# Moving the fallback path ahead of the main path, and queries and V per group, in a grouped-query attention kernel

## Chip, cores, metric

One core of one Trainium2 chip. The metric is device microseconds of one execution, median over several; faster or slower needs 2%. Engines: PE does matmuls, ACT the exps, DVE evicts results, POOL copies V, SP issues the DMAs. The "issue" of a DMA is the time that its record on SP lasts; it has "landed" when its data are there.

## The reference

```python
B, Hq, Hkv, Sq, Sk, D = 16, 32, 8, 288, 512, 128          # bf16
k = jnp.repeat(k, 4, axis=1); v = jnp.repeat(v, 4, axis=1)
scores = jnp.einsum("bhqd,bhkd->bhqk", q, k) * D ** -0.5
p = softmax(scores)
return jnp.einsum("bhqk,bhkd->bhqd", p, v)
```

There are 128 groups (16 x 8): each has 1152 query rows (9 tiles of 128), 512 keys, and takes three steps.

## The kernel before

The main path takes exp without subtracting the maximum. It gathers the range of the row sums, and at the end a flag says whether they are in bounds. If not, all engines run a general path (the fallback; 11,150 PE instructions in the built program) that subtracts it. Here the flag is 0.

```python
def op_load(u, part=None):                # u: unit of UG = 4 groups, 3 slots
    ...                                   # wait until the slot's scores are done
    eng.dma_start_transpose(kt_sb[...], k_v[(gg + g0) * P:(gg + g1) * P])
    eng.dma_start_transpose(qt_sb[...], q_v[(gg + g0) * P:(gg + g1) * P])
    if part != 0:
        ...
        eng.dma_start(vd_sb[:, sl], v_v[:, gg:gg + UG])

def op_s(n):    # a step of PE: 4 matmuls, 1536 columns of scores, 2 buffers in PSUM
    ...
def op_exp(n):  # ACT: exp of 128x1536
    ...
def op_pv(r):   # PE, NC + 1 = 4 steps later: 12 matmuls 128x129 (V and a ones column)
    ...
def op_vc(u):   # POOL: spreads a unit's V (128x2048) beside the ones column
    ...
sp.append((-10.0, lambda: op_load(0, 0)))          # group 0
sp.append((-9.0, lambda: op_load(0, 1)))           # groups 1 to 3
for u in range(1, NU):
    sp.append((-8.0 if u < NSLOT else NC * UG * (u - NSLOT + 1) + LAG, lambda u=u: op_load(u)))
for g in range(NG):
    sp.append((NC * (g + 1) + LAG + 1.5, lambda g=g: op_store(g)))
sp.sort(key=lambda x: x[0])                        # the order of SP's queue
...
def guarded(key, first=None):                      # after the main path, on each engine
    def body(eng):
        eng.wait_ge(sem["s_flag"], 1)
        reg = eng.alloc_register("bad_" + key)
        eng.load(reg, flag_i[:])
        with eng.If_ne(reg, 0):                    # taken jump over the general path
            ...
            fns[key](eng)
```

All DMAs are issued by SP in one queue.

## Time and profile before

| what | value |
|---|---|
| time, median of the first 3 runs | 545.61 us (544.48 to 546.3) |
| profiled span | 542.7 us |
| PE, ACT busy | 524.6 us (97%), 522.0 us (96%) |
| start of the first exp / of the last | 7.37 / 531.40 us |
| from the end of the flag's CAST to the end | 4.9 us |

Two engines at 96% and 97% leave a few microseconds at each end. So one reads when the exp stream starts, whether it is broken, and what follows the flag; the prediction shows those lines. In a windows row the DMA share can pass 1 (1.09 from 20 to 40 us): it is the sum of packet times over 16 engines.

### The profile page before, as it was taken

The page shows a single profiled execution, that of the slowest core. Times are in us where ns is not written, and L with a number is a line of the kernel's source. Part 1 is how long each engine was busy: PE and PEld are TensorE (multiplying, and loading weights), DVE is VectorE, ACT ScalarE, POOL GpSimd, SP SyncE. Part 2 cuts the span into 40 slices and gives each one's busy share as a digit, 9 for nine tenths or more (in the row PEclk, how much of TensorE's full clock was granted, in tenths as well). Part 3 has the DMA queues.
Part 4 walks back from the last instruction along what each step waited for, and adds up shares of the span by engine and source line. Part 5 has one row for each costly group of instructions (what it writes and reads, how often), then busy time and mean ns, then how long its engine had stood idle before and what let it go on. Part 6 is the DMA issues. An engine that isn't in the chain of part 4 may idle for free.

```text
span 542.7 us, 14127 instructions
## 1 busy us (share of the span) xinstructions
PE 524.6 (97%) x6146; PEld 411.1 (76%) x6146; DVE 288.2 (53%) x807; ACT 522.0 (96%) x386; POOL 61.3 (11%) x37
## 2 busy tenths in 40 slices
PE   4799999999999999999999999999999999999994
PEld 1677777777777777777777777777777777777773
DVE  0355555555555555555555555555555555555554
ACT  4799999999999999999999999999999999999992
POOL 0211111011111011111011111001111011111000
PEclk9899999999999999999999999999999999999998
DMA  8999899988879989789998979988888998888211
GB/s 169 214 255 263 212 210 229 206 205 182 236 213 223 213 182 230 205 215 221 192 223 190 229 213 220 246 161 234 183 226 217 198 220 196 223 209 222 88 67 72
DMA packets 250501, 110.05 MB, mean 203 GB/s; under 512 B 217664, under 2 KB 234048, under 8 KB 250432
## 3 DMA queue, kind: packets, MB, share of 16 engines
q1 hardware_dynamic: 250432, 109.07, 84.4%
q8 instruction: 50, 0.82, 0.7%
q14 instruction: 19, 0.16, 0.1%
HBM read 16.78 MB, written 37.75 MB: 100 GB/s over the span
## 4 chain that ended last, share of the span: by engine, by line
PE 95%; SPq 2%; DMA 1%; DVE 1%; POOL 0%; issue 0%
PE ps_o L449 50%; PE ps_s L431 46%; SPq L393 1%; DMA vd_sb<-in_v_dram 1%; SPq L390 1%; POOL v_sb L473 0%; DVE o_sb L493 0%; DVE rl_sb L481 0%; PE ps_s L534 0%; DVE ck_sb L560 0%; DVE ck_sb L566 0%; DVE ck_sb L563 0%; DVE st_sb L505 0%; DVE flag_i L569 0%; DVE st_sb L503 0%
## 5 line engine op out<-in xcount | busy, mean ns | idle before, releaser
L462 ACT ACTIVATE pt_sb<-ps_s 128x1536 bf16<-128x1536 f32 x384 | 520.5, 1451 | 10.1 <-PE ps_s L431 10.0
L449 PEld LDWEIGHTS ps_o<-v_sb,pt_sb 128*128 128x128 bf16 x4608 | 301.0, 98 | 58.7 <-POOL v_sb L473 3.3
L449 PE MATMUL ps_o<-v_sb,pt_sb 128*128 128x129 bf16 x4608 | 333.8, 221 | 3.3 <-POOL v_sb L473 2.9
L431 PE MATMUL ps_s<-qt_sb,kt_sb 128*128 128x512 bf16 (+3 forms) x1536 | 314.1, 327 | 7.9 <-DMA qt_sb<-in_q_dram 7.6
L493 DVE TENSOR_TENSOR o_sb<-ps_o,rl_sb 128x384 bf16<-128x384 f32 x384 | 213.9, 557 | 13.5 <-DVE rl_sb L481 0.3
L481 DVE RECIPROCAL rl_sb<-ps_o 128x3 f32<-128x3 f32 x384 | 69.3, 181 | 234.7 <-PE ps_o L449 234.7
L431 PEld LDWEIGHTS ps_s<-qt_sb,kt_sb 128*128 128x128 bf16 x1536 | 130.0, 98 | 65.7 <-DMA qt_sb<-in_q_dram 5.9
L473 POOL COPY v_sb<-vd_sb 128x2048 bf16<-128x2048 bf16 x32 | 60.7, 1898 | 439.7 <-DMA vd_sb<-in_v_dram 285.7
L505 DVE TENSOR_REDUCE st_sb<-rl_sb 128x1 f32<-128x72 f32 x16 | 3.5, 218 | 0.0
L503 DVE TENSOR_REDUCE st_sb<-rl_sb 128x1 f32<-128x72 f32 x16 | 3.5, 217 | 0.0
L540 ACT ACT_TABLE_LOAD x1 | 1.3, 1283 | 0.8 <-PEq L608 0.8
L534 PE MATMUL ps_s<-ck_sb,one_f 128*1 128x1 f32 x2 | 0.2, 164 | 1.8 <-DVE ck_sb L566 1.8
L534 PEld LDWEIGHTS ps_s<-ck_sb,one_f 128*1 128x1 f32 x2 | 0.1, 82 | 2.0 <-DVE ck_sb L566 2.0
L552 DVE MEMSET dum<- 128x2 f32 x1 | 0.1, 60 | 0.9 <-PEq L608 0.9
L546 POOL MEMSET v_sb<- 128x48 bf16 x1 | 0.3, 312 | 0.3 <-POOLq L608 0.3
L569 DVE CAST flag_i<-ps_s 1x1 int32<-1x1 f32 x1 | 0.1, 145 | 0.3 <-PE ps_s L534 0.3
L540 ACT ACTIVATE dum<-dum 128x1 f32<-128x1 f32 x1 | 0.2, 203 | 0.0
L560 DVE TENSOR_REDUCE ck_sb<-st_sb 128x1 f32<-128x16 f32 x1 | 0.2, 170 | 0.0
L566 DVE SCALAR_TENSOR_TENSOR ck_sb<-ck_sb 128x1 f32<-128x1 f32 x1 | 0.2, 158 | 0.0
L563 DVE TENSOR_SCALAR ck_sb<-ck_sb 128x1 f32<-128x1 f32 x1 | 0.2, 153 | 0.0
L562 DVE TENSOR_REDUCE ck_sb<-st_sb 128x1 f32<-128x16 f32 x1 | 0.2, 159 | 0.0
L608 POOL MEMSET const-float32-0.0<- 128x1 f32 x1 | 0.1, 100 | 0.3 <-issue 0.3
(4 smaller groups left out, 0.4 us busy)
## 6 DMA issues: line engine op xcount, KB each, us to landing
out_dram<-o_sb SPq DMA_DIRECT2D x128, 288.0 KB, 4.9
vd_sb<-in_v_dram SPq DMA_DIRECT2D x32, 512.0 KB, 4.8
kt_sb<-in_k_dram SPq DMA_TRANSPOSE x33, 5.1
qt_sb<-in_q_dram SPq DMA_TRANSPOSE x33, 8.4
```

The costliest lines, as they stand in the source:

```text
L390: eng.dma_start_transpose(kt_sb[:, sl, :, g0:g1].rearrange("d j g p -> d j (g p)"), k_v[(gg + g0) * P:(gg + g1) * P]).then_inc(sk, 16)
L393: eng.dma_start_transpose(qt_sb[:, sl, :, g0:g1].rearrange("d t g p -> d t (g p)"), q_v[(gg + g0) * P:(gg + g1) * P]).then_inc(sq, 16)
L431: ins = emit(eng, waits if x == 0 else [], lambda: eng.matmul(ps_s[:, n % 2, a - i * CH:b - i * CH], kt_sb[:, sl, j, gi, :], qt_sb[:, sl, ...
L449: ins = emit(eng, waits if a == 0 and j == 0 else [], lambda: eng.matmul(ps_o[:, r % 2, a * DV:(a + 1) * DV], w, v_sb[:, sl, gi * NJ + j, ...
L462: emit(eng, waits, lambda: eng.activation(pt_sb[:, g % NPT, i * CH:(i + 1) * CH], ps_s[:, n % 2], ACTF.Exp, scale=scale)).then_inc(sem["s_ ...
L473: emit(eng, waits, lambda: eng.tensor_copy(v_sb[:, sl, :, 0:D], vd_sb[:, sl].rearrange("p g (j d) -> p (g j) d", d=D))).then_inc(sem["s_vc ...
L481: emit(eng, [("s_pv", r + 1)], lambda: eng.reciprocal(rl_sb[:, 3 * r:3 * r + 3], src.rearrange("p a e -> p (a e)"))).then_inc(sem["s_rc"], 1)
L493: emit(eng, waits, lambda: eng.tensor_tensor(out=o_sb[:, g % NO, t0:t0 + 3, :], in0=src, in1=rl_sb[:, 3 * r:3 * r + 3].unsqueeze(2).broadc ...
L503: emit(eng, [("s_rc", (b + 1) * w // 3)], lambda: eng.tensor_reduce(st_sb[:, 0, b:b + 1], rl_sb[:, b * w:(b + 1) * w], AX.X, ALU.max))
L505: eng.tensor_reduce(st_sb[:, 1, b:b + 1], rl_sb[:, b * w:(b + 1) * w], AX.X, ALU.min).then_inc(sem["s_stat"], 1)
L534: emit(eng, [("s_bad", 1)], lambda: eng.matmul(ps_s[0:1, 0, 0:1], one_f[:], ck_sb[:, 3:4], start=True, stop=True)).then_inc(sem["s_bad"], 1)
L540: emit(eng, [("s_one", 1)], lambda: eng.activation(dum[:, 1:2], dum[:, 0:1], ACTF.Exp))
```

## The change

The intent: (1) put the general path ahead of the main path in each engine's stream, so that the engines jump at the start, while they wait for data anyway, and run straight to the end after the flag; (2) transpose queries per group (12 slots) and spread V per group, so that work starts with less loaded; (3) let SP read the flag before it waits for the last stores.

```diff
+        def behind_general(key, first=None):
+            def body(eng):
+                home[key] = nc.cur_bb
+                eng.br("main_" + key)
+                with nc.body("general_" + key):
+                    ...
+                    fns[key](eng)
+                    eng.br("done_" + key)
+                nc.switch_bb("main_" + key)
+        def end(eng, key):
+            eng.wait_ge(sem["s_flag"], 1)
+            eng.load(reg, flag_i[:])
+            if key == "sp":
+                ...                        # the waits for the last stores
+            eng.br_ne(reg, 0, "general_" + key, "done_" + key)
-        qt_sb = ... [P, NSLOT, NT, UG, P]
+        qt_sb = ... [P, NQ, NT, P]          # NQ = 12
-        def op_load(u, part=None):          # K, queries and V of a unit
+        def op_kv(u, part=None):            # K and V of a unit
+        def op_q(g):                        # queries of one group
+            if g >= NQ: ...                 # wait for the scores of group g - 12
+            eng.dma_start_transpose(qt_sb[:, g % NQ], q_v[g * P:(g + 1) * P])
+            sp.append((NC * UG * (u - 1) - 1.0 if u < NSLOT else ..., lambda u=u: op_kv(u)))
+            sp.append((-9.5 if g == 0 else -8.5 + 0.1 * g if g < UG else NC * (g - NQ + 1) + 1.2, lambda g=g: op_q(g)))
-            for u in range(NU): op_vc(u)
+            for g in range(NG): op_vc(g)
```

More of the change, by code (lines that the diff above doesn't have):

```diff
@@ L314, in bass_standalone__gqa_softmax__near_ridge_kernel @@
     NSLOT = 3
+    NQ = 12
     NPT = 3
@@ L333, in bass_standalone__gqa_softmax__near_ridge_kernel @@
         block = es.enter_context(nc.Block())
+        S("s_go")
+        gen = ExitStack()
+        fns = general_path(nc, gen, q, k, v, out, sem["s_go"])
+        gen.close()
+        home = {}
+        def behind_general(key, first=None):
+            def body(eng):
+                if first:
+                    first(eng)
+                home[key] = nc.cur_bb
+                eng.br("main_" + key)
+                with nc.body("general_" + key):
+                    if key == "sp":
+                        eng.sem_inc(sem["s_go"], 1)
+                    fns[key](eng)
+                    eng.br("done_" + key)
+                nc.switch_bb("main_" + key)
+            return body
+        def end(eng, key):
+            eng.wait_ge(sem["s_flag"], 1)
+            reg = eng.alloc_register("bad_" + key)
+            eng.load(reg, flag_i[:])
+            if key == "sp":
+                for g in range(NG - NO, NG):
+                    for (s, n) in need(eng, [("s_o%d" % (g % NO), 16 * (g // NO + 1))]):
+                        eng.wait_ge(s, n)
+            eng.br_ne(reg, 0, "general_" + key, "done_" + key)
+            nc.switch_bb("done_" + key, parent=home[key])
         main = ExitStack()
@@ L336, in bass_standalone__gqa_softmax__near_ridge_kernel @@
         v_sb = main.enter_context(nc.sbuf_tensor("v_sb", [P, NSLOT, UG * NJ, VP], BF16))
-        qt_sb = main.enter_context(nc.sbuf_tensor("qt_sb", [P, NSLOT, NT, UG, P], BF16))
+        qt_sb = main.enter_context(nc.sbuf_tensor("qt_sb", [P, NQ, NT, P], BF16))
         kt_sb = main.enter_context(nc.sbuf_tensor("kt_sb", [P, NSLOT, NJ, UG, P], BF16))
@@ L368, in emit, with PVS @@
             return ins
-        for name in ["s_one", "s_s", "s_e", "s_pv", "s_rc", "s_ev", "s_stat", "s_bad", "s_flag", "s_go", "s_q0", "s_k0", "s_vc"]:
+        for name in ["s_one", "s_s", "s_e", "s_pv", "s_rc", "s_ev", "s_stat", "s_bad", "s_flag", "s_k0", "s_vc"]:
             S(name)
         for i in range(NSLOT):
-            for name in ["s_q%d", "s_k%d", "s_v%d"]:
-                S("u" + name % i)
+            S("us_k%d" % i)
+            S("us_v%d" % i)
+        for i in range(NQ):
+            S("s_q%d" % i)
         for i in range(NO):
             S("s_o%d" % i)
-        def op_load(u, part=None):
+        def PVS(g):
+            return NC * g
+        def op_kv(u, part=None):
             eng = nc.sync
@@ L382, in op_load @@
             if u >= NSLOT:
-                last = (u - NSLOT + 1) * UG - 1
-                for (s, n) in need(eng, [("s_s", NC * (last + 1))]):
+                for (s, n) in need(eng, [("s_s", NC * UG * (u - NSLOT + 1))]):
                     eng.wait_ge(s, n)
             g0, g1 = {None: (0, UG), 0: (0, 1), 1: (1, UG)}[part]
-            sq = sem["s_q0"] if part == 0 else sem["us_q%d" % sl]
-            sk = sem["s_k0"] if part == 0 else sem["us_k%d" % sl]
             gg = u * UG
@@ L391, in op_load @@
                 kt_sb[:, sl, :, g0:g1].rearrange("d j g p -> d j (g p)"),
-                k_v[(gg + g0) * P:(gg + g1) * P]).then_inc(sk, 16)
-            eng.dma_start_transpose(
-                qt_sb[:, sl, :, g0:g1].rearrange("d t g p -> d t (g p)"),
-                q_v[(gg + g0) * P:(gg + g1) * P]).then_inc(sq, 16)
-            if part != 0:
-                if u >= NSLOT:
-                    for (s, n) in need(eng, [("s_vc", u - NSLOT + 1)]):
-                        eng.wait_ge(s, n)
-                eng.dma_start(
-                    vd_sb[:, sl], v_v[:, gg:gg + UG]).then_inc(sem["us_v%d" % sl], 16)
+                k_v[(gg + g0) * P:(gg + g1) * P]).then_inc(sem["s_k0" if part == 0 else "us_k%d" % sl], 16)
+            if part == 1:
+                return
+            if u >= NSLOT:
+                for (s, n) in need(eng, [("s_vc", UG * (u - NSLOT + 1))]):
+                    eng.wait_ge(s, n)
+            eng.dma_start(
+                vd_sb[:, sl], v_v[:, gg:gg + UG]).then_inc(sem["us_v%d" % sl], 16)
+        def op_q(g):
+            eng = nc.sync
+            if g >= NQ:
+                for (s, n) in need(eng, [("s_s", NC * (g - NQ + 1))]):
+                    eng.wait_ge(s, n)
+            eng.dma_start_transpose(qt_sb[:, g % NQ], q_v[g * P:(g + 1) * P]).then_inc(sem["s_q%d" % (g % NQ)], 16)
         def op_store(g):
@@ L421, in op_s @@
             waits = []
-            if g == 0:
-                waits += [("s_k0", 16), ("s_q0", 16)]
-            else:
-                waits += [("us_k%d" % sl, 16 * (u // NSLOT + 1)), ("us_q%d" % sl, 16 * (u // NSLOT + 1))]
+            waits.append(("s_k0", 16) if g == 0 else ("us_k%d" % sl, 16 * (u // NSLOT + 1)))
+            waits.append(("s_q%d" % (g % NQ), 16 * (g // NQ + 1)))
             if n >= 2:
@@ L433, in op_s @@
                     kt_sb[:, sl, j, gi, :],
-                    qt_sb[:, sl, r0 // P:(r0 + b - a) // P, gi, :], start=True, stop=True))
+                    qt_sb[:, g % NQ].rearrange("d t p -> d (t p)")[:, r0:r0 + b - a], start=True, stop=True))
             ins.then_inc(sem["s_s"], 1)
@@ L441, in op_pv @@
             sl = u % NSLOT
-            waits = [("s_vc", u + 1), ("s_e", NC * (g + 1))]
+            waits = [("s_vc", g + 1), ("s_e", NC * (g + 1))]
             if r >= 2:
@@ L460, in op_exp @@
             if g >= NPT:
-                waits.insert(0, ("s_pv", NC * (g - NPT + 1)))
+                waits.insert(0, ("s_pv", PVS(g - NPT + 1)))
             emit(eng, waits, lambda: eng.activation(
@@ L464, in op_exp, with op_vc @@
             ).then_inc(sem["s_e"], 1)
-        def op_vc(u):
+        def op_vc(g):
             eng = nc.gpsimd
+            u, gi = g // UG, g % UG
             sl = u % NSLOT
@@ L471, in op_vc @@
             if u >= NSLOT:
-                waits.append(("s_pv", NC * UG * (u - NSLOT + 1)))
+                waits.append(("s_pv", PVS(g - NSLOT * UG + 1)))
             emit(eng, waits, lambda: eng.tensor_copy(
-                v_sb[:, sl, :, 0:D], vd_sb[:, sl].rearrange("p g (j d) -> p (g j) d", d=D))
+                v_sb[:, sl, gi * NJ:(gi + 1) * NJ, 0:D], vd_sb[:, sl, gi].rearrange("p (j d) -> p j d", d=D))
             ).then_inc(sem["s_vc"], 1)
@@ L510, in bass_standalone__gqa_softmax__near_ridge_kernel @@
         sp, pe = [], []
-        sp.append((-10.0, lambda: op_load(0, 0)))
-        sp.append((-9.0, lambda: op_load(0, 1)))
+        sp.append((-10.0, lambda: op_kv(0, 0)))
+        sp.append((-9.0, lambda: op_kv(0, 1)))
         for u in range(1, NU):
-            sp.append((-8.0 if u < NSLOT else NC * UG * (u - NSLOT + 1) + LAG, lambda u=u: op_load(u)))
+            sp.append((NC * UG * (u - 1) - 1.0 if u < NSLOT else NC * UG * (u - NSLOT + 1) + LAG, lambda u=u: op_kv(u)))
+        for g in range(NG):
+            sp.append((-9.5 if g == 0 else -8.5 + 0.1 * g if g < UG else NC * (g - NQ + 1) + 1.2, lambda g=g: op_q(g)))
         for g in range(NG):
@@ L520, in _ @@
         def _(eng):
+            behind_general("sp")(eng)
             for (_, fn) in sp:
                 fn()
-            for g in range(max(0, NG - NO), NG):
-                for (s, n) in need(eng, [("s_o%d" % (g % NO), 16 * (g // NO + 1))]):
-                    eng.wait_ge(s, n)
+            end(eng, "sp")
         @block.tensor
         def _(eng):
+            behind_general("pe")(eng)
             for n in range(NS + LAG):
@@ L536, in _ @@
             ).then_inc(sem["s_bad"], 1)
+            end(eng, "pe")
         @block.scalar
         def _(eng):
+            behind_general("act")(eng)
             emit(eng, [("s_one", 1)], lambda: eng.activation(dum[:, 1:2], dum[:, 0:1], ACTF.Exp))
@@ L542, in _ @@
                 op_exp(n)
+            end(eng, "act")
         @block.gpsimd
         def _(eng):
+            behind_general("pool")(eng)
             eng.memset(v_sb[:, :, :, D:DV], 1.0)
-            for u in range(NU):
-                op_vc(u)
+            for g in range(NG):
+                op_vc(g)
+            end(eng, "pool")
         @block.vector
         def _(eng):
+            behind_general("dve")(eng)
             eng.memset(dum[:], 0.0).then_inc(sem["s_one"], 1)
@@ L570, in _ @@
                  ).then_inc(sem["s_flag"], 1)
+            end(eng, "dve")
         main.close()
-        gen = ExitStack()
-        fns = general_path(nc, gen, q, k, v, out, sem["s_go"])
-        def guarded(key, first=None):
-            def body(eng):
-                eng.wait_ge(sem["s_flag"], 1)
-                reg = eng.alloc_register("bad_" + key)
-                eng.load(reg, flag_i[:])
-                with eng.If_ne(reg, 0):
-                    if first:
-                        first(eng)
-                    fns[key](eng)
-            return body
-        block.sync(guarded("sp", lambda eng: eng.sem_inc(sem["s_go"], 1)))
-        block.tensor(guarded("pe"))
-        block.scalar(guarded("act"))
-        block.vector(guarded("dve"))
-        block.gpsimd(guarded("pool"))
-        gen.close()
 _INS = ['q', 'k', 'v']
```

## The prediction

> **What bounds the kernel now.** I read the page first (busy shares and groups), then a table of windows, then both ends of the timeline, then the queue's own waits. The page puts PE at 97% and ACT at 96%, so the group rows decide:
>
> ```profile
> L462 ACT ACTIVATE pt_sb<-ps_s 128x1536 bf16<-128x1536 f32 x384 | 520.5, 1451 | 10.1 <-PE ps_s L431 10.0
> L431 PE MATMUL ps_s<-qt_sb,kt_sb 128*128 128x512 bf16 (+3 forms) x1536 | 314.1, 327 | 7.9 <-DMA qt_sb<-in_q_dram 7.6
> L473 POOL COPY v_sb<-vd_sb 128x2048 bf16<-128x2048 bf16 x32 | 60.7, 1898 | 439.7 <-DMA vd_sb<-in_v_dram 285.7
> ```
>
> 384 exps cover 520.5 us, 1.355 us each; ACT idles 10.1 us ahead of them in the whole run. Where is that idle time? The windows say:
>
> ```profile
> 0.00:20.00 20.00, 9.21 (x49) 4.98 (x50) 0.83 (x4) 9.76 (x8) 2.41 (x6) 0.92 0.91 186
> 20.00:40.00 20.00, 20.00 (x236) 15.60 (x234) 11.07 (x30) 19.36 (x16) 3.80 (x2) 1.00 1.09 237
> 200.00:300.00 100.00, 100.00 (x1184) 78.76 (x1182) 55.41 (x154) 100.00 (x75) 11.39 (x6) 1.00 0.90 213
> ```
>
> Columns: window, its length, busy us of PE, PEld, DVE, ACT, POOL, the granted clock, DMA share and GB/s. From about 21 us on ACT is busy without a break. In the records the exps there start 1.354 us apart (median), 1.348 even where an exp had its scores waiting, so the middle is held by exp; the matmuls follow it. Nothing in the diff changes an exp. Only the ends can move.
>
> The start, on the DMA queue and on ACT:
>
> ```profile
> 0.81 1.31 SPq L390 DMA_TRANSPOSE kt_sb<-in_k_dram  x1
> 2.18 1.35 SPq L393 DMA_TRANSPOSE qt_sb<-in_q_dram  x1
> 3.57 1.50 SPq L390 DMA_TRANSPOSE kt_sb<-in_k_dram  x1
> 5.12 4.58 SPq L393 DMA_TRANSPOSE qt_sb<-in_q_dram  x1
> 9.74 0.58 SPq L400 DMA_DIRECT2D vd_sb<-in_v_dram  x1
> ...
> 7.37 4.32 ACT L462 ACTIVATE pt_sb<-ps_s 128x1536 bf16<-128x1536 f32 x3 [5.07 <-PE ps_s L431]
> 12.78 2.79 ACT L462 ACTIVATE pt_sb<-ps_s 128x1536 bf16<-128x1536 f32 x2 [1.09 <-PE ps_s L431]
> 18.76 1.45 ACT L462 ACTIVATE pt_sb<-ps_s 128x1536 bf16<-128x1536 f32 x1 [3.19 <-PE ps_s L431]
> 20.85 1.45 ACT L462 ACTIVATE pt_sb<-ps_s 128x1536 bf16<-128x1536 f32 x1 [0.64 <-PE ps_s L431]
> ```
>
> The first exp starts at 7.37, the seventh at 20.85. Unbroken it would be 7.37 + 6 x 1.354 = 15.49, so 5.36 us are lost: to the transpose of three groups' queries (landing 11.8) and to V, issued behind it (landing 14.3, whole copy of 1.90 us, first P*V at 16.3). The run is thus as if an unbroken exp stream had begun at 12.73.
>
> The end: the last exp starts at 531.40, then come the last P*V, the flag, and
>
> ```profile
> 537.63 0.14 DVE L569 CAST flag_i<-ps_s 1x1 int32<-1x1 f32 x1 [0.28 <-PE ps_s L534]
> ```
>
> ```profile
> SPq L525 <- DMA out_dram<-o_sb: 1.6, 1, 1.6
> SPq L324 <- PEq L324: 2.8, 1, 2.8
> ```
>
> After the flag, 542.66 - 537.77 = 4.9 us pass in which no engine computes. The second fence is the queue's own waits: its wait for the last stores ends at 538.5 already, but at the closing barrier (L324) it stands 2.8 us waiting for the other engines. In the records these read the flag from 537.81 to about 538.35, branch, and reach the barrier at 541.76 (PE), 541.99 (ACT), 542.06 (POOL) and 542.38 (DVE). PE's branch record alone lasts 3.33 us. SP, whose skipped block is only 110 instructions, goes from its branch at 539.28 to the barrier in 0.47 us.
>
> [...]about 3.5 us for the four engines that jump over 1153 to 11150 instructions, 0.47 us for SP over 110. [...]an issue of a transpose takes 1.31 us for 128 KB and 1.35 us for 288 KB. [...]0.5 is granted from 16.76 to 20.17, after PE stood from 13.4 to 16.3.
>
> **The change, part by part.**
>
> *General path in front.* In the built streams each engine now jumps once at the start over its general block, and at the end runs straight from its branch (not taken) to the closing barrier. End: [...]The last store, issued at 536.45, lands at 538.49; SP now reads the flag before it waits for the stores, so it passes its branch at about 538.6, and with 0.2 us to its barrier entry and the 0.27 us that the barrier took after its last arrival the end falls at about 539.1 instead of 542.66: -3.5 us. Start: PE, ACT, DVE and POOL [...]ready at 0.75 + 3.6 = 4.4; ACT then loads its table (1.28) and is ready near 5.9, ahead of the first scores. Free. SP jumps over 110 instructions: +0.4 us, on the path.
>
> *Queries per group, 12 slots.* The intent is to ask only for what is needed next. But the sort key 3(g-11)+1.2 is applied to every group from 4 on, and for g = 4 to 7 it gives -19.8, -16.8, -13.8 and -10.8, all below the -10 of the first keys. The built stream shows it: four query transposes come first, then K of group 0, V, the queries of group 0, K of groups 1 to 3, group 8, groups 1, 2, 3. Chain: SP starts at 0.81 + 0.4 = 1.2; four issues of 1.35 to 6.6; K 1.31 to 7.9; V 0.58 to 8.5; then the queries of group 0, which in the run before landed 3.65 us after their issue began: 12.15. First exp 1.5 us after that as before (5.88 to 7.37): 13.65.
>
> What follows should be nearly unbroken. V (512 KB, ahead of these queries) lands near 12 and its first copy is a quarter as long (512 of 2048 elements, about 0.5 us); P*V is not asked for until the fifth score step. The queries of group 1 are issued two transposes later, 8.5 + 1.35 + 1.50 + 1.35 = 12.7, landing near 16.4; their scores can start once the second exp is done, 13.65 + 2 x 1.35 + 0.17 = 16.5. I allow 0.2 us (a half-clock step, as the 1.52 interval before). The stream begins effectively at 13.85 instead of 12.73: +1.1 us. So the start that was to be shortened gets longer, by less than the 6.3 us of delay in the first exp, because the old gaps of 5.36 go.
>
> *V copies per group.* 128 copies of a quarter instead of 32. POOL is 11% busy, so nothing beyond the start.
>
> *Middle.* Queries are asked for some 32 steps (43 us) ahead. Four issues of 1.35 take 5.4 us where the one before took 5.46 (median of the tile view); bytes are the same. Zero.
>
> Sum: 545.61 + 1.1 - 3.5 = 543.2 us.
>
> **Rivals.** (1) [...]its 0.47 us at the old end speaks against; if so, +3 us, about 546. (2) The order of the start costs more: backlog behind V pushes the queries of group 0 to 14, or group 1 stalls as well; DMA share of 0.9 to 1.09 in the first 40 us speaks for some of it, but four issues 1.35 us apart move 218 KB/us, less than the 250 to 290 KB/us that the packets of the queries reached around 10 and 18 us. +2 us, 545. (3) The intended start really wins: if the early transposes cost only their issue and later groups profit, or the second half-clock stretch that now vanishes is worth more; 541 to 542. (4) Finer DMAs disturb the steady stretch: the queue waits 198.5 us on results to store, so it has slack; a step of 1.354 that grew by 0.5% would add 2.6 us. (5) Another wait takes the end, for instance the last store's 2.05 us landing: already counted.
>
> **Range and chances.** Gain at the end 3 to 4, loss at the start 0 to 4, spread of the runs before about 1 either way: 540.5 to 546.3. A change of 2% is 10.9 us; all that is not exp at both ends is 542.7 - 520.5 = 22 us, and no path above moves half of it. Faster by over 2%: 0.02, within 2%: 0.96, slower: 0.02.
>
> **What would show it.** Queue: four query transposes ahead of the first K, first at about 1.2. First matmul near 12, first exp near 13.7, then no ACT gap over 0.5 us; no second half-clock stretch. Middle steps of 1.354. After the flag's CAST some 1.3 us to the end instead of 4.9, with no long wait of the queue at the barrier. I am wrong [...]if the first exp comes after 16[...].

The sum came to 545.61 + 1.1 - 3.5 = 543.2 us. The four engines took 3.4 to 4.0 us from their branches (538.30 to 538.39) to the barrier (541.76 to 542.38); the -3.5 is worked out from the last store, and the 3.6 us that the four jumps should take at the start is the author's estimate from those waits. Rival (1) was that SP's jump takes as long as theirs. Two signs of being wrong were a late issue of the first K and a jump's wait left behind the flag. The allowance of 0.2 us is an estimate from the 1.52 us between the second exp and the third: a matmul of 512 columns took 0.43 us there, against 0.215 in the middle (the clock has no record before 9.93).

## The result, and the profile after

The changed kernel took 547.68 us (547.06 to 548.3, 4 runs) against 545.26 us for the one before (4 runs): ratio 1.0043, interval 1.002 to 1.0066. Ratios are the mean time of one kernel's fast runs over that of the other's of the same rounds, so not quite the ratio of the quoted medians. That is within 2%, as predicted, but on the other side and outside the range of 540.5 to 546.3. The difference is clear of noise, but only 0.4%.

The DMA queue at the start of the changed kernel, from its timeline (start and length in us, engine, line, operation; the first line is from a shorter window, which shows the first issue alone):

```profile
1.26 6.63 SPq L445 DMA_TRANSPOSE qt_sb<-in_q_dram  x1
...
1.26 11.28 SPq L445 DMA_TRANSPOSE qt_sb<-in_q_dram  x4
12.58 1.27 SPq L429 DMA_TRANSPOSE kt_sb<-in_k_dram  x1
13.89 0.58 SPq L437 DMA_DIRECT2D vd_sb<-in_v_dram  x1
14.53 1.29 SPq L445 DMA_TRANSPOSE qt_sb<-in_q_dram  x1
```

Its ACT, from two windows of the same view (the last row is cut off where its window ends, near 60 us):

```profile
5.06 1.28 ACT L587 ACT_TABLE_LOAD   x1 [5.06 <-issue]
6.35 0.20 ACT L587 ACTIVATE dum<-dum 128x1 f32<-128x1 f32 x1
20.59 40.41 ACT L504 ACTIVATE pt_sb<-ps_s 128x1536 bf16<-128x1536 f32 x30 [14.04 <-PE ps_s L473]
```

Its end, from the timeline and from the queue's own waits:

```profile
545.13 0.15 DVE L620 CAST flag_i<-ps_s 1x1 int32<-1x1 f32 x1 [0.28 <-PE ps_s L579]
```

```profile
SPq L327 <- PEq L327: 0.2, 1, 0.2
```

The end did what it should: 1.1 us from the CAST to the end at 546.4 instead of 4.9, and 0.2 us at the barrier instead of 2.8. After its start the exp stream has no gap, and the engines that jump are ready at 5.06, far ahead of the data. But four query transposes go first, as the built order said, and the first of them alone holds the queue for 6.63 us. The first exp starts at 20.59 where I had 13.65. The balance of the spans: the exp stream, counted back from its last start by 383 x 1.354 us, begins effectively at 20.32 instead of 12.82 (12.73 by the prediction's count), +7.5; the end gives -3.75; and 542.66 + 7.5 - 3.75 = 546.4. Each profile is of one execution: the one of the kernel before took 544.39 us, less than its four timed runs, and the one of the changed kernel 548.3, the slowest of its four. So the spans differ by 3.75 us, the medians of the times by 2.4.

Two questions were open: why an issue of 1.35 us took 6.63, and what each part of the change is worth.

### The profile page after: what moved, and what is told of

Its sections match the earlier page's. It is cut to its first block, busy times and chain, and to the rows that moved or that the text cites. A ratio compares the mean times of both kernels' runs of the same rounds, so it can differ in the third digit from the quotient of the medians.

```text
span 546.4 us, 14512 instructions
## 1 busy us (share of the span) xinstructions
PE 522.8 (96%) x6146; PEld 410.2 (75%) x6146; DVE 288.6 (53%) x807; ACT 521.2 (95%) x386; POOL 73.6 (13%) x133
## 4 chain that ended last, share of the span: by engine, by line
PE 95%; SPq 2%; DMA 1%; ACT 1%; DVE 1%; issue 0%
PE ps_o L491 49%; PE ps_s L473 45%; SPq L445 2%; DMA qt_sb<-in_q_dram 1%; ACT pt_sb L504 1%; DVE o_sb L536 0%; SPq L429 0%; SPq L437 0%; DVE rl_sb L524 0%; PE ps_s L579 0%; DVE ck_sb L617 0%; DVE ck_sb L611 0%; DVE ck_sb L614 0%; DVE flag_i L620 0%; DVE st_sb L548 0%
## 5 line engine op out<-in xcount | busy, mean ns | idle before, releaser
L516 POOL COPY v_sb<-vd_sb 128x512 bf16<-128x512 bf16 x128 | 73.1, 616 | 424.7 <-DMA vd_sb<-in_v_dram 369.7
```

The costliest lines, as they stand in the source:

```text
L516: emit(eng, waits, lambda: eng.tensor_copy(v_sb[:, sl, gi * NJ:(gi + 1) * NJ, 0:D], vd_sb[:, sl, gi].rearrange("p (j d) -> p j d", d=D))). ...
```

## The experiments

Eleven kernels ran, and all passed the check of the result, even the last, which computes a wrong result (see e11). "First issue" is the first DMA issue on SP; "after flag" is from the CAST's end to the end of the span. Starts, lengths and spans (us) are from the records of one profiled execution each; times are medians of 4 to 6 runs. The time of the kernel before beside them was 544.73 us (e1 to e4), 544.41 (e5 to e8) and 544.60 (e9 to e11), with single runs from 542.30 to 545.86. As the flag is 0 for these inputs, no run took the general path. "Front" names the engines whose general path is ahead; order "new" is the changed kernel's.

| run | front | order | first issue | first exp | after flag | span | time | ratio to before |
|---|---|---|---|---|---|---|---|---|
| before | none | old | 1.31 | 7.37 | 4.88 | 542.7 | 545.26 | 1 |
| changed | all | new | 6.63 | 20.59 | 1.13 | 546.4 | 547.68 | 1.0043 |
| e1 | all | key mended | 5.58 | 13.57 | 1.14 | 542.3 | 543.88 | 0.9991 |
| e2 | all | old | 5.34 | 12.25 | 1.13 | 543.9 | 544.97 | 1.0003 |
| e3 | none | new | 1.36 | 15.21 | 5.30 | 545.5 | 546.97 | 1.0047 |
| e4 | all but SP | new | 1.36 | 16.97 | 1.57 | 543.5 | 544.74 | 1.0006 |
| e5 | SP | new | 3.08 | 17.42 | 4.92 | 547.3 | 548.85 | 1.0079 |
| e7 | all, SP's block cut | new | 2.69 | 17.83 | 1.14 | 544.0 | 545.51 | 1.0014 |
| e6 | all but SP | paced | 1.32 | 10.11 | 1.56 | 536.7 | 538.17 | 0.9879 |
| e8 | none | paced | 1.32 | 7.73 | 5.30 | 538.0 | 539.40 | 0.9907 |
| e10 | all | paced | 4.68 | 12.00 | 1.14 | 538.2 | 540.22 | 0.9923 |
| e9 | all but SP, DVE and POOL jump late | paced | 1.32 | 9.70 | 1.57 | 536.1 | 537.91 | 0.9880 |

### e1: the sort key mended, nothing else

```diff
-(-9.5 if g == 0 else -8.5 + 0.1 * g if g < UG else NC * (g - NQ + 1) + 1.2)
+(-9.5 if g == 0 else -8.5 + 0.1 * g if g < UG else 0.5 * (g - UG) if g < NQ else NC * (g - NQ + 1) + 1.2)
```

> The changed kernel, with one sort key mended so that the query transposes of groups 4 to 11 come after what the first groups need (no query transpose ahead of the first K). Theory F (two separate losses: the four early query transposes cost about 6 us of issue[...]): the first issue, now that of K, still lasts about 6.6 us, the first exp starts at about 14.5 instead of 20.59, the span is about 540.4. Rival Q (the first issue is long because it is a query transpose of the new form, or because four of them follow each other): the first issue is back at 1.3 us, first exp at about 9.3, span about 535.

The second loss of theory F was that the start jumps of the four other engines lengthen the queue's first issue, to 6.63 us instead of 1.31.

The first issue, now of K, still lasted 5.58 us: rival Q fell. The first exp came at 13.57, sooner than theory F's 14.5. Yet the span is 542.3 and not 540.4. The reason is in its waits (engine, line, what it waited for: total us, times, longest), and in the queue's timeline, which follows:

```profile
DVE o_sb L536 <- DMA out_dram<-o_sb: 4.6, 2, 3.4
PE ps_o L491 <- DVE o_sb L536: 2.6, 3, 2.2
```

```profile
32.55 5.77 SPq L445 DMA_TRANSPOSE qt_sb<-in_q_dram  x3
38.36 0.58 SPq L451 DMA_DIRECT2D out_dram<-o_sb  x1
```

The timeline shows the first store behind the eagerly issued transposes, at 38.36, some 25 us after the first exp. With six output buffers the eviction then waits for a store, and PE for the eviction: two exp intervals, after the 28th and the 34th exp, are 1.62 and 3.72 us instead of 1.354. Asking for queries 11 groups ahead is not free.

### e2: the kernel before with the general path in front only

```diff
 (kernel before)
+  behind_general(key) ahead of each engine's main path, end(eng, key) after it
-  guarded(key)
```

> The kernel before, with only the general path moved in front (and the new end with it); loads and V copies as before. Theory F: the first issue lasts about 6.6 us, the first exp starts at about 13.1 instead of 7.37, and after the flag 1.1 us remain instead of 4.9: span about 544.6. Rival Q: first issue 1.3 us, first exp at about 7.8, span about 539.3.

The queue's timeline in e2, first two issues:

```profile
1.27 5.34 SPq L421 DMA_TRANSPOSE kt_sb<-in_k_dram  x1
6.66 1.35 SPq L424 DMA_TRANSPOSE qt_sb<-in_q_dram  x1
```

A first issue of 5.34 us without any new query transpose: the placement alone makes it long. The 3.75 us won at the end are more than paid for at the start (first exp +4.9 us, the later gaps about the same): the span grows by 1.2 us, and the time cannot be told from that of before (0.9964 to 1.0041).

### e3: the changed kernel with every general path behind

```diff
+            if key not in FRONT:           # FRONT = ()
+                with eng.If_ne(reg, 0):
+                    ...
+                    fns[key](eng)
+                return
```

> The changed kernel with the general path of every engine behind the main path again (four query transposes still first). Theory F: first issue 1.35 us, first exp at about 14.9, the end after the flag back at about 4.9 us; span about 544.4. Rival Q: first issue still about 6.6 us, span about 549.7.

First issue 1.36 us and first exp at 15.21, close to theory F; the span of 545.5 is 1.1 us above its 544.4, with 5.30 us after the flag instead of 4.9 and 0.3 us lost ahead of the third exp. The order of the loads alone is therefore worth this much: against e8 below, which differs in the order and pacing of the loads alone, 15.21 - 7.73 = 7.5 us.

### e4 and e5: SP alone behind, SP alone in front

```diff
-FRONT = ()
+FRONT = ("pe", "act", "dve", "pool")      # e4
+FRONT = ("sp",)                           # e5
```

> The changed kernel with the general path behind for the queue's engine SP alone; PE, ACT, DVE and POOL still jump at the start. [...]the first issue still lasts about 6.6 us, from 0.81 on, first exp at about 20.1, span about 546. If SP's own jump does it (rival S): first issue 1.35 us, first exp at about 14.9, span about 541.

The first figures are those of theory F: that the four others' jumps are enough for the long issue.

The queue's timeline in e4, the first issue and the second (two short windows):

```profile
0.81 1.36 SPq L454 DMA_TRANSPOSE qt_sb<-in_q_dram  x1
```

```profile
2.23 2.23 SPq L454 DMA_TRANSPOSE qt_sb<-in_q_dram  x1
```

My theory F fell here: with SP's code not jumping, the first issue is 1.36 us although the four others still jump. Their jumps only stretch the second issue to 2.23 us (1.39 in e3) and the fourth to 2.73 (1.72), together with smaller delays +1.76 us at the first exp. So SP's own jump is needed. Rival S had left this stretch out: its span of 541 was 2.5 us too low.

> The changed kernel with the general path in front for SP alone (behind for PE, ACT, DVE and POOL), four query transposes still first. Theory S (SP's own jump over its general block costs the queue's first issue its 5.3 us): first issue about 5 to 6.6 us, first exp at about 20[...]: span about 549. Rival C[...]: first issue under 3.5 us, first exp at about 15.5 to 17, span 545 to 547.

Rival C was that the long issue needs the jumps of the four others beside SP's own. The first span also counts their wait at the end.

The queue's timeline in e5, first issue:

```profile
1.26 3.08 SPq L454 DMA_TRANSPOSE qt_sb<-in_q_dram  x1
```

But it isn't enough either: alone it makes the first issue 3.08 us, not 6.63. With the first exps one gets a table of two by two, order "new" throughout: nobody in front 15.21; the others alone 16.97 (+1.76); SP alone 17.42 (+2.21); all 20.59 (+5.38), 1.4 us more than the two added. That is rival C of the expectation: SP's jump has a delay of its own, which grows when four other engines jump at the same time. The first exp at 17.42 and the span of 547.3 are both just above what I wrote for C (15.5 to 17, 545 to 547).

### e7: SP's general block cut to a stub

```diff
-                    fns[key](eng)
+                    if key != "sp":
+                        fns[key](eng)
```

> The changed kernel with SP's general block cut to its semaphore increment and branch (its loads left out; the flag is 0 for these inputs, so the result must stay right, but as a fallback it would be broken). If the distance of SP's jump matters[...]: first issue 1.35 us, first exp at about 17, as with SP behind, span about 542.9. If any jump on SP at this place does it, or the position of SP's code does not matter: first issue still 5 to 6.6 us, first exp at about 20.5, span about 546.4.

The queue's timeline in e7, first issue:

```profile
0.95 2.69 SPq L446 DMA_TRANSPOSE qt_sb<-in_q_dram  x1
```

With next to nothing to jump over, the first issue takes 2.69 us, not 6.63, and the first exp comes at 17.83; the span of 544.0 lies between the two expectations. It is not the 1.36 and 16.97 of SP behind, so a short jump still costs 0.9 us at the first exp. The cut shortens the jump and also shifts where the rest of SP's code lies; this run does not separate the two.

The packets say more. From the start of the first issue to the first packet of data pass 1.42 us in before and e4, 1.43 in e7, but 3.13 in e5 and 4.49 to 4.89 in e1, e2, e10 and the changed kernel. So in e7 data flow as early as without a jump, and only the rest of the issue is long, as that of e4's second is. And the profile labels the packets of two queues, q8 and q14, as "instruction". Their rows in the DMA view of the first 20 us, for q14, in the changed kernel, e7 and e5:

```profile
q14 instruction: 7, 0.06, 1.1%
q14 instruction: 6, 0.05, 0.9%
q14 instruction: 1, 0.01, 0.1%
```

With SP's jump over its 110 instructions beside the four others q14 has 7 packets (e1, e2 and e10 too), with SP behind or its block cut 6 (e4, e6 and e7), with SP alone 1; before, e3 and e8 have none. On q8 there are 2 wherever the four others jump in the first 20 us, and none in e5. One packet more goes with the late start of the data.

### e6 and e8: the order mended and paced, SP behind; and the same with all behind

```diff
+        sp.append((-8.35, lambda: op_kv(0, 2)))     # V of unit 0 on its own, after queries of group 1
-(-9.5 if g == 0 else -8.5 + 0.1 * g if g < UG else NC * (g - NQ + 1) + 1.2)
+(-9.5 if g == 0 else -8.5 + 0.1 * g if g < UG else NC * (g - 5) + 0.2)
+FRONT = ("pe", "act", "dve", "pool")      # e6;  () in e8
```

> The version that the runs point to: SP's general path behind, the others' in front; K and queries of group 0 first, then K of groups 1 to 3, queries of 1, V, queries of 2 and 3; later queries asked for 5 groups ahead instead of 11, so that stores do not queue behind them. If the loss is the order and SP's jump: first exp at about 8.5, no ACT gap over 0.5 us later, end 1.7 us after the flag, span about 535.5, ratio to before about 0.988. If [...]stores still come late: first exp past 10 or gaps near steps 27 and 33 as in e1, span 538 or more.

The condition was that the four others' jumps still delay the queue.

The timeline of e6, the queue's first issues:

```profile
0.81 1.32 SPq L439 DMA_TRANSPOSE kt_sb<-in_k_dram  x1
2.18 2.18 SPq L455 DMA_TRANSPOSE qt_sb<-in_q_dram  x1
4.41 1.78 SPq L439 DMA_TRANSPOSE kt_sb<-in_k_dram  x1
6.24 2.67 SPq L455 DMA_TRANSPOSE qt_sb<-in_q_dram  x1
8.95 0.58 SPq L447 DMA_DIRECT2D vd_sb<-in_v_dram  x1
```

and ACT's exps from the third on:

```profile
13.12 12.20 ACT L514 ACTIVATE pt_sb<-ps_s 128x1536 bf16<-128x1536 f32 x9 [0.21 <-PE ps_s L483]
```

538.17 us, ratio 0.9879 (interval 0.9858 to 0.99): better than both kernels, though short of the 2% that would count as faster. After the first exp ACT's only gap is 0.21 us, ahead of the third; from the twentieth on no interval passes 1.36 us, so the stalls of e1 are gone. The first exp came at 10.11, not 8.5: the jumps of the four other engines stretch the issue of the first queries to 2.18 us and that of group 1's to 2.67 (1.35 and 1.87 in e8), and the expectation's alternative ("first exp past 10") holds in that.

> e6 with the general path of all engines behind. If the placement in front is worth its end without its start: first exp 0.5 to 1.8 us earlier than e6, the end after the flag 4.9 instead of 1.7 us: span 1.5 to 3 us longer than e6. [...]

The alternative: the others' jumps cost as much at the start as at the end, and the span stays the same.

The queue's timeline in e8, second and fourth issue:

```profile
2.18 1.35 SPq L455 DMA_TRANSPOSE qt_sb<-in_q_dram  x1
5.14 1.87 SPq L455 DMA_TRANSPOSE qt_sb<-in_q_dram  x1
```

Without any jump the first exp is at 7.73, 2.38 us earlier than in e6 (I had written 0.5 to 1.8); the end after the flag is 5.30, 3.74 us longer. The span of e6 is 1.36 us shorter, just under my 1.5 to 3. The times differ by about as much (538.17 to 539.40). The intervals of the two ratios to before overlap, but these kernels ran side by side and their single runs do not (537.34 to 538.45 and 539.19 to 539.96): the gain of the placement is real here, and small, 0.2%. About three quarters of the gain over before is in e8 already (0.93% of 1.21% by the ratios): queries and V per group, in a good order and pacing; no run separates these from one another.

### e9: DVE and POOL jump late

```diff
+            behind_general("pool", lambda eng: eng.wait_ge(sem["s_k0"], 16))(eng)
+            # DVE: its memset of dum first, then the same wait, then the jump
```

> e6, with DVE and POOL waiting for the first K (landing near 4 to 5 us) before they jump[...]. [...]the second issue (queries of group 0) back from 2.18 to about 1.4 to 1.8 us, first exp at 8.5 to 9.3 instead of 10.11, span about 535.5. [...]first exp at about 10 or a gap after it, span 536.7 or more.

The first figures are for two jumps instead of four beside the first issues and a stretch in proportion to their number; the second for two that stretch as much as four, or for late ones that stretch the issues of group 1.

The second issue went from 2.18 to 1.96 us and the first exp from 10.11 to 9.70; 537.91 us, ratio 0.9880, the same as e6. Nearer the alternative than the main guess, and not worth its code. The difference is hardly more than chance: e11 below, whose start is that of e6, has 2.35 us and 10.17. So how the stretch goes with the number of jumps stays open.

### e10: all in front, paced

```diff
 (e6)
-FRONT = ("pe", "act", "dve", "pool")
+FRONT = ("sp", "pe", "act", "dve", "pool")
```

> The changed kernel with all general paths in front, in the order and pacing of e6: the only difference to e6 is SP's own jump. Theory C[...]: first issue 5.3 to 5.6 us as in e1 and e2, first exp at about 12.5 to 13 instead of 10.11, no gaps later, span 538 to 539. If a good order makes the jump harmless: first exp at about 10.5, span about 536.5.

Theory C is rival C of e5: SP's jump delays its first issue more beside the four others.

The queue's timeline in e10, first two issues:

```profile
1.26 4.68 SPq L430 DMA_TRANSPOSE kt_sb<-in_k_dram  x1
6.00 1.93 SPq L446 DMA_TRANSPOSE qt_sb<-in_q_dram  x1
```

First issue 4.68 us and first exp at 12.00, both somewhat under what I wrote (5.3 to 5.6, 12.5 to 13); the first exp is 1.89 us after that of e6, the span 1.55 us longer. After the third exp no gap, with SP in front as in e1: so e1's gaps came from order and pacing and not from where SP's code lies.

### e11: who holds the middle

The exps of the changed kernel had a surprise: in the first fifteen steps they start 1.330 us apart, and only then 1.354. If exp were the bound of the middle, as I had predicted, it could not go faster at the start.

```diff
 (e6)
-pt_sb[:, g % NPT, i * CH:(i + 1) * CH], ps_s[:, n % 2], ACTF.Exp
+pt_sb[:, g % NPT, i * CH:i * CH + (CH if g < NPT else 1024)], ps_s[:, n % 2, 0:CH if g < NPT else 1024], ACTF.Exp
```

> e6 with the exp of groups 3 and later over 1024 of its 1536 columns (a wrong result on purpose: the rest of the tile keeps older values). If PE holds the middle at 1.354 us a step, as the first 15 steps of the changed kernel suggest (exp 1.330 apart until it has caught up with PE): step still about 1.354, span about 536.7. If exp holds it, as I predicted from the exps without a break: the step falls to about 1.33 or less, span below 529.

Windows view of e11 (window, length, busy us of PE, PEld, DVE, ACT, POOL, clock, DMA share, GB/s), and its group row of the exp (busy and mean ns; then idle time):

```profile
100.00:200.00 100.00, 100.00 (x1184) 78.75 (x1182) 55.47 (x154) 75.49 (x75) 13.71 (x24) 1.00 0.97 213
```

```profile
L514 ACT ACTIVATE pt_sb<-ps_s 128x1024 bf16<-128x1024 f32 (+1 forms) x384 | 395.8, 1033 | 127.9 <-PE ps_s L483 127.8
```

The output is wrong, though the check of the result passed it: by an estimate from the reference's inputs (0.05 times a normal) the scaled scores spread by only 0.0025 about zero, so every exp is near 1 and older values pass for it. ACT now idles a quarter of the time and waits for PE's scores, and the step is still 1.354 us, the span 536.7 as in e6, the time 538.44. PE holds the middle. In the changed kernel's records its matmuls start 58.8 ns apart in P*V and 151 and 198 ns within and after the scores: 12 x 58.8 + 3 x 150.6 + 197.6 = 1355 ns. ACT could go at 1.330, 24 ns a step faster.

## Why the prediction was wrong

Point by point, by its own steps.

**The end, right.** -3.5 us predicted, -3.75 measured. From their branches to the barrier the four engines now take 0.07 to 0.15 us instead of 3.4 to 4.0, and SP's wait there went from 2.8 to 0.2 us.

**The order of the load issues, right in kind.** The built stream had the four transposes first, and e3 shows their cost without jumps. The prediction misread one place in it: the queries of groups 1, 2 and 3 (keys -8.4 to -8.2) come ahead of those of group 8 (-7.8), not behind. It made no difference, as the second exp, at 16.5 by its chain, bound the scores of group 1.

**"SP jumps over 110 instructions: +0.4 us, on the path": the step that failed.** I took it from SP's 0.47 us at the old end. The branch itself did take that long again (0.46 us), but the first DMA issue behind it then lasted 6.63 us instead of 1.35, +5.28. At the old end only a few closing instructions followed the same jump, so it could not show what the next DMA issue would pay. e4 shows that without SP's jump the issue is normal, e5 that with SP's jump alone it is 3.08, e7 that with the block cut the data start as early as without a jump. Rival (1) named a longer jump of SP and put it at 3 us; I gave it too little room, because I took a wait seen beside the closing barrier for the cost of the jump as such.

**The other terms of the start.** From 13.65 to 20.59 there are 6.94 us: 5.28 the first issue, 0.06 its start, 0.69 the later issues up to that of group 0's queries, 0.87 their landing (4.52 us after the issue began, not 3.65: in that time the transposes issued at 10.98 and 12.58 landed, at 15.15 and 15.87, and V at 18.03), 0.04 the first step. "Ready near 5.9. Free" held for ACT itself (ready at 6.55), but not for the queue: the others' jumps stretched SP's issues (e4, +1.76 us). The chain left that stretch out: the second issue lasts 2.23 us in e4, 1.39 in e3.

**The middle, wrong in its cause.** "The middle is held by exp" is refuted by e11. It did no harm to the sum, as the step did not change: "Zero" for the middle held (1.354 before and after). That was luck in part, since the change does alter what PE's score matmuls read. The sign that I had at hand and misread was the 1.348 of exps whose scores were there: they were faster than the 1.354 of the rest, so these were waiting. The chain that ended last also put 95% of the span on PE's two lines of matmuls.

**The range.** The two losses were each in the list of rivals, at +3 and +2, but not together. Added to my 543.2 they give 548.2, near the measured 547.68, but with sizes that are not those of the trace: 5.3 us for the first and 1.6 (0.69 + 0.87) for the second. Two of the prediction's own signs of being wrong came: the first K was issued late, at 12.58, and the first exp came after 16.

**What stays open.** The runs show that a jump on SP delays its first issue (1.36 us without it, 3.08 with it alone, 6.63 beside four other jumps), and that with the block that it jumps over cut the data start 1.43 us after the issue began instead of 4.49 to 4.89 (e7). What holds the issue in between is not shown. Instruction packets move beside the jumps, but not only there: in the first 20 us of the changed kernel 2 on q8 and 7 on q14, of before none; from 537 to 542 us of before, where its engines jump, 1 and 4, and in the 100 us from 100 on, where none jumps, 9 and 2. Which packet belongs to which engine, and whether an engine waits for one, the profile does not say. Whether the distance or the place of SP's later code counts is not separated. Why SP's first issue lasts 3.6 us longer beside four other jumps than alone (6.63 to 3.08) isn't settled.

## What to carry to other kernels

Code moved out of the end of a stream may be paid for where it goes, as here: look at which engine issues the first transfers, and leave that one's stream straight (e6 against e10: first exp at 10.11 and 12.00, 538.17 and 540.22 us). When the order of a queue comes from a sort key, print the built order, and check the key's values for the first few indices, where a formula meant for the steady state goes negative; then ask how far ahead to load, since requests too early hold up stores behind them in the same queue (e1: the first store at 38.36 us, two exp intervals of 1.62 and 3.72 us instead of 1.354). Two engines at 97% and 96% do not tell which one holds the other: shrink one engine's work and see whether the step moves (e11: 1.354 us still, with exps over 1024 of 1536 columns).
